# Joint Gram products of keys and queries in fewer TensorE visits, and masks and norms of the start handed to GpSimd

## The chip, the cores and the metric

The kernel runs on one core of a Trainium2 chip. The metric is the device time of one execution in microseconds (us), lower is better.

## The reference, cut to what matters

A linear attention with a delta rule runs over 768 time steps of 4 x 8 heads of size 48. Its output, 3072 rows of 384, goes through two feed-forward blocks one after the other ("MoE 1" with a product of two up projections, "MoE 2" with a leaky rectifier).

```python
for t in range(S):                       # attention, per batch b and head h
    kt, vt, bt = (k_n[:, :, t], v[:, :, t], beta[:, :, t, None])    # k_n: keys over their norms
    y[:, :, t] = np.einsum('bhd,bhde->bhe', q[:, :, t], state)
    v_old = np.einsum('bhde,bhd->bhe', state, kt)
    state = state + bt[:, :, :, None] * np.einsum('bhd,bhe->bhde', kt, vt - v_old)
x = y.transpose(0, 2, 1, 3).reshape(B * S, H * D)
x = (x @ w_a * (x @ w_b)) @ w_out                                   # MoE 1, 384 -> 1536 -> 384
h = x @ w_in                                                        # MoE 2, 384 -> 2048 -> 384
out = (np.maximum(h, 0.0) + alpha * np.minimum(h, 0.0)) @ w_out2
```

## The kernel before

**Stages.** Time is cut into six chunks (`c`, `NSC = 6`) of 128 time steps, each of two steps (`j`) of 64 time steps. In a chunk the recurrence becomes dense algebra for 32 (batch, head) pairs, 16 on each half of the partitions (`x`). A chunk `N` that comes next needs:

- `norms`: reciprocal norms of the keys, a chain of small operations over 128x32 elements (`ss`, `s`, `r` and `b` in the trace);
- `masks`: for each `j` the tile `mb`, 128x1024, beta times a triangular mask;
- Gram products `g` of keys with keys, masked into `ef`, and of keys with queries, masked into the rows of `Z` that `yp` reads later;
- `fold` (ScalarE copies in `ef`), then the triangular inversion (a transpose `eu<-ef` and a long chain of short VectorE operations on `inv`, `itmp`, `eu`), `diagonal` (transposes into `hw` and `TT`) and `offdiag` (32x32 products `w` and `xx`).

Then `step` runs once for each `j`: products `rp` (keys with the state) and a subtraction into `v`; products `up` and ScalarE copies into `SU`; products `sp` and a subtraction into the next `SU`; products `yp`, whose banks are split into `x`, the input of MoE 1. `up` and `sp` are done in two halves of eight heads, each half a "visit" of its own.

**Order of the work.** Chunk 0's attention and the inversions of chunks 0 and 1 come first; MoE 1 of chunk 0 starts once its `x` is there. From then on MoE 1 of chunk `c - 1` (128x512 matmuls `p` and `o`) runs on TensorE, and the small products of attention chunk `c` break into it, a visit at a time. The Gram products of chunk `c + 1` ride in the visits of `up` and `sp` as "mates" (`mate`): in the step of `j = 0` four visits take the key Grams of all heads, in the step of `j = 1` four visits take the query Grams. After chunk 5 come the rest of MoE 1 and MoE 2 (`h`, `o`). Operations are recorded first; `Schedule` then lists them greedily by engine, taking at each moment, of the operations that its cost table says are ready, the one with the longest path behind it. Consecutive small matmuls form one task; so a visit starts when the inputs and the banks of all its products are there.

**Engines.** Large matmuls take weights `wu`, which VectorE, ScalarE and GpSimd first decode (`raw`, `e`, `W`) and split in two (`wu`); the hidden activations `a` are split into `g` by ScalarE and GpSimd. Small products are 32-bit matmuls on tiles of the array: rows by the half of the partitions that is read, columns by the half of the bank that is written. Each shows as two MATMUL instructions in the trace, so that the eight heads of an `up` visit show as 32.

**Banks.** `chain` has two banks, `pre` and `g` one each. Mates use `chain` in chunk 1 and `pre` from chunk 2 on.

**What the change and the rows touch.** In the start: `A.masks(L, 0, ..., nc.vector)`, `A.masks(N, 0, ..., nc.vector)` and `A.norms(N, ef1)`, with `L` chunk 0 and `N` chunk 1. In the loop over `c`: `mate`, `step`, and the place of the third part of `norms` and of `masks`, which before stood inside the first step. In chunk 1 (`c == 1`, `direct` false) ScalarE copied the query Grams to `Z` and GpSimd masked them; from chunk 2 on VectorE did both in one operation per half.

Of the kernel before, what the change touches and what calls it, by code (L numbers as in the profile page):

```python
# [5 lines left out]
F32 = mybir.dt.float32  # L6
# [216 lines left out]
class Schedule:  # L223
# [24 lines left out]
    def costs(s, t):  # L248
        op, k = t.ops[0], len(t.ops)
        size = max(v.ix.size for v in ([op.dst] if op.dst is not None else []) + [v for v in op.src if v.ix.size < 2048])  # L250
        name = op.dst.tile.kw.get("name") if op.dst is not None else None
        t.rows = op.dst.p if op.dst is not None else None
        if t.dma:
            moved = op.dst if op.dst is not None else op.src[0]
            n = moved.ix.size * (moved.p[1] - moved.p[0])
            t.cost, t.lag = 0.42 if t.eng == SP_ else 0.1, 0.05 + n / (9.8e4 if name == "raw" else 6.5e4)
        elif t.eng == PE_:
            if t.large:
                t.cost = {512: 0.2267, 256: 0.12}[op.dst.ix.size]
            elif op.name == "transpose":  # L260
                t.cost = 0.09 * k
            else:
                rows = {0: 0.0, 1: 0.0}
                for x in t.ops:
                    a, b = x.src[0].p
                    for g in range(a // 64, (b + 63) // 64):
                        rows[g] += 0.00085 * x.src[0].ix.shape[-1]
                t.cost = max(0.0172 * k, *rows.values())
            t.lag = t.cost + 0.25
        elif t.eng == ACT_:  # L270
            t.lag = 0.16 + 0.00082 * size if any(map(in_psum, op.src)) else 0.19 + 0.00083 * size
            t.cost = t.lag + 0.02
        elif t.eng == POOL_:
            t.lag = 0.2 + 0.0007 * size
            if op.name == "tensor_tensor":
                t.lag = {32: 0.27, 384: 1.0, 512: 1.27, 768: 1.48, 1024: 1.91, 1536: 2.77}[size]
# [174 lines left out]
class Attention:  # L451
# [50 lines left out]
    def bank(s, name, tag="chain"):  # L502
        return s.pools[tag].tile([128, 512], F32, tag=tag, name=name, bufs=BANKS[tag])
# [95 lines left out]
            products(i)  # L599
        return g  # L600

    def mate(s, L, j, i8, tag, queries, then=None, direct=True):

        def begun():
            g, products = s.grams(L, j, i8, tag, *((1, 2) if queries else (0, 0)), go=False)

            def keep():
                if queries and direct:
                    s.mask_queries(L, j, i8, g, s.nc.vector)
                elif queries:  # L610
                    s.keep_queries(L, j, i8, g)
                    s.spend(ACT, 5)
                    s.mask_queries(L, j, i8, None, s.nc.gpsimd)
                else:
                    s.mask_keys(L, j, i8, g)
                    s.spend(DVE, 3)
                if then is not None:
                    then()

            return products, keep  # L620

        return begun
# [130 lines left out]
                    s.spend(ACT, 1.5)  # L753
            yield

    def step(s, c, j, L, mates=(), joined=False):

# [16 lines left out]

        if st > 0:
            rp = [bank("rp") for _ in halves]
            for i in range(8):
                for h, (o, _) in enumerate(halves):  # L780
                    near, far = slice(64 * h, 64 * h + 64), slice(64 - 64 * h, 128 - 64 * h)
                    nc.tensor.matmul(rp[h][near, i, :], Z[64:112, 0, o + i, :], SU[0][64:112, o + i, 0:48], start=True, stop=True)
                    nc.tensor.matmul(rp[h][far, i, :], Z[0:48, 0, o + i, :], SU[1][0:48, o + i, 0:48], start=True, stop=True)
            nc.vector.tensor_tensor(R[:, 0:8, :], rp[0], R[:, 0:8, :], ALU.subtract)
            s.spend(DVE, 2.3)
            if not joined:
                yield
            for x in range(2):
                sl, other = slice(64 * x, 64 * x + 64), slice(64 - 64 * x, 128 - 64 * x)
                nc.vector.tensor_tensor(R[sl, 8:16, :], rp[1][other], R[sl, 8:16, :], ALU.subtract)  # L790
                s.spend(DVE, 2.3)
            yield
        for o, hs in halves:
            up = bank("up")
            beside, keep = mate()
            for i in range(8):
                for x in range(2):
                    sl = slice(64 * x, 64 * x + 64)
                    nc.tensor.matmul(up[sl, i, :], s.TT[sl, j, o + i, :], R[sl, o + i, :], start=True, stop=True)
                beside(i)  # L800
            for x in range(2):
                sl = slice(64 * x, 64 * x + 64)
                nc.scalar.copy(SU[x][sl, hs, 0:48], up[sl])
                s.spend(ACT, 1.9)
            keep()
            yield
        for o, hs in halves:
            if st == 2 * NSC - 1:
                break
            sp = bank("sp")  # L810
            beside, keep = mate()
            for i in range(8):
                for x in range(2):
                    sl = slice(64 * x, 64 * x + 64)
                    nc.tensor.matmul(sp[64 * x : 64 * x + 48, i, :], bk[sl, j, o + i, :], SU[x][sl, o + i, 0:48], start=True, stop=True)
                beside(i)
            nc.vector.tensor_tensor(SN[1][0:48, hs, 0:48], SU[0][64:112, hs, 0:48], sp[0:48], ALU.subtract)
            s.spend(DVE, 4.4)
            nc.vector.tensor_tensor(SN[0][64:112, hs, 0:48], SU[1][0:48, hs, 0:48], sp[64:112], ALU.subtract)
            keep()  # L820
            yield
        tag = "chain" if c else "ab"
# [24 lines left out]
def attn_moe_kernel(tc, kt, qt, kn, vn, beta, w_a, w_b, w_o, w_in, w_o2, alpha, out):  # L847
    nc = tc.nc
    with ExitStack() as ctx:
# [249 lines left out]
        N = A.load(1)  # L1099
        al = cp.tile([128, M2], F32, name="al")  # L1100
        nc.sync.dma_start(al, alpha)
        A.masks(L, 0, wp.tile([128, 16, 64], F32, tag="w9", name="mb0"), nc.vector)
        A.masks(L, 1, xroom(0, 1, [16, 64], F32, "mb1"))
        A.scale_values(L, 0)
        A.clear()
# [25 lines left out]

# [147 lines left out]
        for c in range(NSC):  # L1279
# [3 lines left out]
            if c > 0:  # L1283
# [15 lines left out]
                for i, _ in enumerate(A.offdiag(L)):  # L1299
                    going = run(moe, fill, PIECE) and going  # L1300
                    if N is not None and i == 1:
                        norms = A.norms(N, late=True)
                        next(norms)
                        next(norms)
                mates = [[], []]

                def keys_done():
# [1 line left out]
                    A.scale_keys(N)  # L1309

                if N is not None:
                    after = {(0, 8): lambda: A.fold(N, 0), (1, 8): keys_done}
                    for q in range(2):
                        mates[q] += [A.mate(N, *jg, tag, q == 1, after.get(jg) if q == 0 else None, c > 1) for jg in HALF]
                closed.clear()
                L["y"] = [None, None]
                for j in range(2):
                    for i, _ in enumerate(A.step(c, j, L, mates[j], True)):
                        if N is not None and i == j == 0:
                            next(norms, None)  # L1320
                            A.masks(N, 0)
                            A.masks(N, 1)
# [191 lines left out]
```

## Time and profile before

| what | value |
|---|---|
| median of 3 runs | 1033.73 us (1033.64 to 1033.9) |
| profiled execution, its own time | 1034.53 us |
| its span, first to last instruction | 1032.8 us |
| mean granted TensorE clock | 0.973 of full speed |
| busy: PE, DVE, ACT, POOL | 981.1, 611.1, 480.6, 582.9 us |

PE is TensorE (matmuls), PEld its weight loads, DVE VectorE, ACT ScalarE, POOL GpSimd. In a timeline or a chain each row gives the start in us from the start of the span, the duration in us, the engine, the operation, output<-inputs and the number of instructions; in brackets stands the idle time of the engine before it and what ended it. A merged row of several instructions covers all of them.

### The profile page before, as it was taken

To read this page: it belongs to the slowest core of one execution; us is meant where nothing else is said; L and a number is where in the kernel's file an instruction comes from. 1 tells how busy PE (TensorE), PEld (TensorE's weight loads), DVE (VectorE), ACT (ScalarE), POOL (GpSimd) and SP (SyncE) were. 2 spreads that over 40 slices of the span, in tenths; PEclk is the share of its full clock that TensorE was granted. 3 is DMA by queue.
4 is the path that set the end of the run, shared out by engine and by line. 5 is a ranking of instruction groups with operands and counts; after the bars stand their busy time and mean duration, and the time that the engine had idled before them with its cause. 6 is when DMAs were issued, how large, how long until landed. Compare 5 with 4: busy or idle time off the path is not lost.

```text
span 1032.8 us, 24930 instructions
## 1 busy us (share of the span) xinstructions
PE 981.1 (95%) x10462; PEld 807.6 (78%) x10462; DVE 611.1 (59%) x1182; ACT 480.6 (47%) x963; POOL 582.9 (56%) x514
## 2 busy tenths in 40 slices
PE   6077999999999999999999999999999999999998
PEld 5076877887788788778878888888888888888886
DVE  8999766863684578358628799534343343433333
ACT  4386887565457554745567887212121121211211
POOL 7457999968466756756545998333333333333332
PEclk9559999999999999999999999999999999999999
DMA  9514343201300220000013751002020010000000
GB/s 249 182 42 139 110 145 111 78 1 34 95 32 2 63 95 1 18 19 32 16 35 98 235 172 62 31 1 62 0 62 1 1 62 1 28 4 1 31 0 31
DMA packets 26943, 61.47 MB, mean 60 GB/s; under 512 B 4304, under 2 KB 8912, under 8 KB 26832
## 3 DMA queue, kind: packets, MB, share of 16 engines
q1 hardware_dynamic: 26400, 59.50, 18.9%
q8 instruction: 82, 1.34, 0.5%
q10 hardware_dynamic: 432, 0.39, 0.1%
q14 instruction: 29, 0.24, 0.1%
HBM read 50.44 MB, written 9.44 MB: 58 GB/s over the span
## 4 chain that ended last, share of the span: by engine, by line
PE 83%; POOL 1%; issue 1%; ACT 0%; DVE 0%; DVEq 0%; POOLq 0%
PE o L201 32%; PE p L201 25%; PE h L201 19%; PE yp L201 2%; PE g L201 1%; PE up L201 1%; PE sp L201 1%; PE rp L201 1%; POOL wu L201 1%; PE xx L201 0%; PE w L201 0%; POOL W L201 0%; POOL g L201 0%; ACT SU L201 0%; ACT Z L201 0%
## 5 line engine op out<-in xcount | busy, mean ns | idle before, releaser
L201 PE MATMUL p<-x,wu 128*128 128x512 f32 x1296 | 321.9, 395 | 3.2 <-DVE a L201 1.3
L201 PEld LDWEIGHTS p<-x,wu 128*128 128x128 f32 x1296 | 239.0, 188 | 56.7 <-DVE a L201 1.7
L201 POOL TENSOR_TENSOR g<-neg,g 128x512 fp32r<-128x512 f32 x95 | 124.2, 1307 | 257.6 <-ACT g L201 257.6
L201 POOL TENSOR_TENSOR wu<-W,wu 128x384 fp32r<-128x384 f32 x195 | 202.1, 1041 | 98.3 <-ACT wu L201 97.2
L201 PE MATMUL o<-g,v 128*128 128x512 f32 x870 | 211.7, 388 | 0.0
L201 PE MATMUL h<-x,v 128*128 128x512 f32 x864 | 211.4, 389 | 0.0
L201 DVE TENSOR_SCALAR neg<-h,al 128x512 f32<-128x512 f32 (+1 forms) x97 | 72.2, 745 | 221.5 <-PE h L201 221.5
L201 ACT CAST g<-neg 128x512 fp32r<-128x512 f32 (+1 forms) x97 | 59.8, 616 | 301.5 <-DVE neg L201 283.9
L201 PEld LDWEIGHTS o<-g,v 128*128 128x128 f32 x870 | 162.4, 188 | 33.8 <-ACT x2s L201 0.5
L201 PEld LDWEIGHTS h<-x,v 128*128 128x128 f32 x864 | 162.2, 188 | 33.7
L201 PE MATMUL o<-g,wu 128*128 128x512 f32 x648 | 164.2, 394 | 0.1
L201 PEld LDWEIGHTS o<-g,wu 128*128 128x128 f32 x648 | 121.7, 189 | 26.8 <-POOL g L201 0.7
L201 ACT CAST wu<-W 128x384 fp32r<-128x384 f32 x216 | 110.2, 514 | 56.6 <-PE o L201 25.8
L201 POOL TENSOR_TENSOR g<-a,g 128x512 fp32r<-128x512 f32 x71 | 93.1, 1311 | 27.9 <-ACT g L201 27.7
L201 PE MATMUL g<-Z 48*64 48x64 f32 x1536 | 62.6, 241 | 34.0 <-DVE ef L201 22.6
L201 PEld LDWEIGHTS g<-Z 48*64 48x64 f32 x1536 | 56.8, 154 | 35.3 <-DVE ef L201 22.9
L201 DVE TENSOR_TENSOR a<-p,a 128x512 f32<-128x512 f32 x72 | 49.3, 685 | 55.2 <-PE p L201 49.4
L201 DVE TENSOR_TENSOR inv<-inv,itmp 128x240 f32<-128x240 f32 (+23 forms) x236 | 69.9, 296 | 13.6 <-ACT inv L201 6.5
L201 ACT COPY a<-p 128x512 f32<-128x512 f32 x72 | 42.2, 586 | 63.9 <-PE p L201 61.5
L201 DVE SCALAR_TENSOR_TENSOR neg<-h,neg 128x512 f32<-128x512 f32 (+1 forms) x97 | 66.5, 686 | 3.3
L201 ACT CAST g<-a 128x512 fp32r<-128x512 f32 x72 | 44.5, 618 | 19.9 <-DVE a L201 19.2
L201 POOL TENSOR_TENSOR f<-f,v 128x384 int32<-128x384 int32 x32 | 38.9, 1224 | 4.5 <-DVE v L201 3.4
(88 smaller groups left out, 960.1 us busy)
## 6 DMA issues: line engine op xcount, KB each, us to landing
v<-in_w_o_dram SPq DMA_DIRECT2D x16, 384.0 KB, 3.2
v<-in_w_in_dram SPq DMA_DIRECT2D x16, 384.0 KB, 3.6
k<-in_kn_dram SPq DMA_DIRECT2D x6, 768.0 KB, 5.3
Z<-in_kt_dram SPq DMA_DIRECT2D x24, 192.0 KB, 4.2
Z<-in_qt_dram SPq DMA_DIRECT2D x24, 192.0 KB, 4.1
raw<-in_w_a_dram SPq DMA_DIRECT2D x12, 384.0 KB, 3.9
v<-in_vn_dram SPq DMA_DIRECT2D x12, 384.0 KB, 3.7
raw<-in_w_b_dram SPq DMA_DIRECT2D x12, 384.0 KB, 4.9
```

The lines of the kernel that those rows point to most:

```text
L201: getattr(s.engines[op.eng], op.name)(*(real(x) for x in op.a), **{w: real(x) for w, x in op.k.items()})
```

## The change

Four parts.

1. `mate` now takes four heads and both Grams at once: one product with the keys as weights (64 columns) and keys beside queries as moving data (128 columns), in place of two with 64 each. There are still eight mates in a chunk, four in the step of each `j`, now with that `j`'s own heads. Behind each, VectorE does three mask operations (128x256 into `ef`, twice 64x256 into `Z`) in every chunk, chunk 1 too.
2. `step(..., wide=True)` from chunk 2 on: a mate rides with `rp`; the halves of `up` share one visit, with a mate; the halves of `sp` share one where there are no mates (chunk 5), else each half keeps its visit and mate. The second half of a joined visit is written to the other column half of its bank, so that four tiles of the array are in use. A step with mates goes from six visits to five, one without to four.
3. In the start the first masks of chunks 0 and 1 go from VectorE to GpSimd, and four operations of chunk 1's norms (`late=True`).
4. The planner gets a cost term for the columns that a tile of the array moves, and a GpSimd cost for 256 elements. Masks and the last part of the norms of the next chunk are recorded before the steps.

```diff
@@ Schedule.costs
-                rows = {0: 0.0, 1: 0.0}
+                rows, tiles = {0: 0.0, 1: 0.0}, {}
                 for x in t.ops:
                     a, b = x.src[0].p
                     for g in range(a // 64, (b + 63) // 64):
                         rows[g] += 0.00085 * x.src[0].ix.shape[-1]
-                t.cost = max(0.0172 * k, *rows.values())
+                        for c in range(x.dst.p[0] // 32, (x.dst.p[1] + 31) // 32):
+                            tiles[g, c] = tiles.get((g, c), 0.0) + 0.00085 * x.dst.ix.size
+                t.cost = max(0.0172 * k, *rows.values(), *tiles.values())
@@ Attention.mate
+            g = s.bank("g", tag).rearrange("p (i w n) -> p i w n", w=2, n=64)
+                for x, rows, both in ((0, slice(64, 112), slice(0, 2)), (1, slice(0, 48), slice(0, 3, 2))):
+                    nc.tensor.matmul(
+                        g[64 * x : 64 * x + 64, i], Z[rows, 0, i4 + i, :], Z[rows, both, i4 + i, :], start=True, stop=True,
+                    )
             def keep():
-                if queries and direct:
-                    s.mask_queries(L, j, i8, g, s.nc.vector)
-                elif queries:
-                    s.keep_queries(L, j, i8, g)
-                    s.mask_queries(L, j, i8, None, s.nc.gpsimd)
-                else:
-                    s.mask_keys(L, j, i8, g)
+                nc.vector.tensor_tensor(L["ef"][:, j * 16 + i4 : j * 16 + i4 + 4, :], g[:, :, 0, :], mb[:, hs, :], ALU.mult)
+                for x in range(2):
+                    nc.vector.tensor_tensor(Z[sl, 1 + x, hs, :], g[sl, :, 1, :], mb[sl, hs, :], ALU.mult)
@@ Attention.step
+            beside, keep = mate() if wide else none          # with rp
-        for o, hs in halves:
+        for group in (halves,) if wide else ((h,) for h in halves):              # up
+                for n, (o, _) in enumerate(group):
+                    for x in range(2):
+                        sl, at = slice(64 * x, 64 * x + 64), 64 * (x ^ n)
+                        nc.tensor.matmul(ups[n][at : at + 64, i, :], s.TT[sl, j, o + i, :], R[sl, o + i, :], start=True, stop=True)
-        for o, hs in halves:
+        for group in (halves,) if wide and not mates else ((h,) for h in halves):   # sp
@@ the start
-        A.masks(L, 0, wp.tile([128, 16, 64], F32, tag="w9", name="mb0"), nc.vector)
+        A.masks(L, 0, wp.tile([128, 16, 64], F32, tag="w9", name="mb0"))
-        norms = A.norms(N, ef1)
+        norms = A.norms(N, ef1, late=True)
-        A.masks(N, 0, xroom(1, 1, [16, 64], F32, "mb0"), nc.vector)
+        A.masks(N, 0, xroom(1, 1, [16, 64], F32, "mb0"))
@@ the loop over chunks
+                if N is not None:
+                    next(norms, None)
+                    A.masks(N, 0)
+                    A.masks(N, 1)
-                        mates[q] += [A.mate(N, *jg, tag, q == 1, after.get(jg) if q == 0 else None, c > 1) for jg in HALF]
+                        mates[q] += [A.mate(N, q, i4, tag, after.get((q, i4))) for i4 in range(0, 16, 4)]
-                    for i, _ in enumerate(A.step(c, j, L, mates[j], True)):
+                    for i, _ in enumerate(A.step(c, j, L, mates[j], True, c > 1)):
```

## Rows read from the trace of the kernel before

**Rows 1.** Busy time by stage: us, busy (instructions) of each engine, clock, DMA.

```profile
core 0: us, PE busy (x) PEld busy (x) DVE busy (x) ACT busy (x) POOL busy (x), PEclk, DMA share, GB/s
26.50:53.30 26.80, 3.60 (x66) 3.42 (x68) 24.86 (x67) 9.39 (x18) 10.88 (x6) 0.53 0.51 170
53.30:88.40 35.10, 26.38 (x935) 24.63 (x932) 32.40 (x75) 25.59 (x55) 22.68 (x20) 0.68 0.29 76
88.40:183.70 95.30, 91.60 (x1459) 72.44 (x1459) 68.42 (x129) 74.74 (x154) 87.73 (x86) 1.00 0.42 128
279.80:373.60 93.80, 93.80 (x1481) 76.01 (x1477) 59.68 (x142) 52.38 (x108) 61.30 (x57) 1.00 0.14 45
```

**Rows 2.** Timeline, first 27 us: VectorE, GpSimd, ScalarE rows of the start.

```profile
9.96 0.19 DVE L201 TENSOR_TENSOR r<-r,ss 128x32 f32<-128x32 f32 x1
...
11.52 1.90 POOL L201 TENSOR_TENSOR mb<-b,mask 128x1024 f32<-128x1024 f32 x1 [3.17 <-DVE b L201]
11.54 2.96 DVE L201 TENSOR_TENSOR mb<-b,mask 128x1024 f32<-128x1024 f32 x1
...
14.61 1.29 DVE L201 TENSOR_TENSOR ef<-g,mb 128x512 f32<-128x512 f32 x2
...
15.81 1.74 DVE L201 TENSOR_REDUCE ss<-ef 128x32 f32<-128x1536 f32 x1
...
17.47 1.27 DVE L201 TENSOR_TENSOR ef<-g,mb 128x512 f32<-128x512 f32 x2
...
19.32 1.24 ACT L201 COPY ef<-ef 32x512 f32<-32x512 f32 x2
...
20.66 2.74 DVE L201 TENSOR_TENSOR r<-r,s 128x32 f32<-128x32 f32 x1
...
23.32 1.94 DVE L201 STREAM_TRANSPOSE eu<-ef 128x1024 f32<-128x1024 f32 x1
```

**Rows 3.** Timeline, 45 to 54 us: VectorE late in the first inversion.

```profile
46.35 2.63 DVE L201 TENSOR_TENSOR mb<-b,mask 128x1024 f32<-128x1024 f32 x1
...
48.91 0.26 DVE L201 TENSOR_TENSOR itmp<-inv,eu 128x108 f32<-128x108 f32 x1
...
53.31 1.94 DVE L201 STREAM_TRANSPOSE hw<-inv 128x1024 f32<-128x1024 f32 x1
```

**Rows 4.** Timeline of TensorE where MoE 1 begins.

```profile
88.41 4.36 PE L201 MATMUL p<-x,wu 128*128 128x512 f32 x18 [0.66 <-DVE x L201]
...
97.40 2.33 PE L201 MATMUL p<-x,wu 128*128 128x512 f32 x9 [1.27 <-DVE a L201]
```

**Rows 5.** Chain that ended last, chunk 5: start, us, what, MATMUL instructions.

```profile
535.15 1.08 PE rp L201 x64
536.23 1.81 PE p L201 x7
538.04 1.06 PE up L201 x32
...
541.04 0.85 PE sp L201 x32
...
551.99 2.00 PE up L201 x64
...
555.80 1.93 PE yp L201 x128
```

**Rows 6.** The same chain in chunk 3: one visit of up with its mate.

```profile
324.81 2.04 PE o L201 x9
...
336.38 0.19 PE up L201 x2
...
337.47 2.27 PE p L201 x9
```

**Rows 7.** Waits of VectorE: us in total, times, longest.

```profile
DVE r L201 <- POOL r L201: 6.1, 3, 2.0
```

**Rows 8.** Groups of instructions by line, whole span: mean ns after the busy us.

```profile
L201 POOL TENSOR_TENSOR Z<-Z,mb 64x512 f32<-64x512 f32 x24 | 30.6, 1275 | 16.6 <-ACT Z L201 15.5
L201 DVE TENSOR_TENSOR Z<-g,mb 64x512 f32<-64x512 f32 x24 | 16.5, 689 | 15.6 <-PE g L201 15.3
```

**Rows 9.** Waits of TensorE: us in total, times, longest.

```profile
PE xx L201 <- issue: 1.0, 1, 1.0
```

**Rows 10.** Busy time by 5 us around that wait, at 234 us.

```profile
230.00:235.00 5.00, 4.21 (x141) 3.33 (x140) 2.40 (x4) 4.57 (x12) 2.67 (x4) 1.00 0.01 3
235.00:240.00 5.00, 4.82 (x15) 3.71 (x15) 1.12 (x3) 3.57 (x9) 4.42 (x7) 0.66 0.02 3
```

More of the change, by code (lines that the diff above doesn't have):

```diff
@@ L275, in costs @@
             if op.name == "tensor_tensor":
-                t.lag = {32: 0.27, 384: 1.0, 512: 1.27, 768: 1.48, 1024: 1.91, 1536: 2.77}[size]
+                t.lag = {32: 0.27, 384: 1.0, 256: 0.74, 512: 1.27, 768: 1.48, 1024: 1.91, 1536: 2.77}[size]
                 t.port = True
@@ L754, in offdiag, with step @@
             yield
-    def step(s, c, j, L, mates=(), joined=False):
+    def step(s, c, j, L, mates=(), joined=False, wide=False):
         nc, ap = s.nc, s.ap
@@ L783, in step @@
                     nc.tensor.matmul(rp[h][far, i, :], Z[0:48, 0, o + i, :], SU[1][0:48, o + i, 0:48], start=True, stop=True)
+                beside(i)
             nc.vector.tensor_tensor(R[:, 0:8, :], rp[0], R[:, 0:8, :], ALU.subtract)
@@ L791, in step @@
                 s.spend(DVE, 2.3)
+            keep()
             yield
-        for o, hs in halves:
-            up = bank("up")
+        for group in (halves,) if wide else ((h,) for h in halves):
+            ups = [bank("up") for _ in group]
             beside, keep = mate()
             for i in range(8):
-                for x in range(2):
[L798 to L804, printed above, removed]
+                for n, (o, _) in enumerate(group):
+                    for x in range(2):
+                        sl, at = slice(64 * x, 64 * x + 64), 64 * (x ^ n)
+                        nc.tensor.matmul(ups[n][at : at + 64, i, :], s.TT[sl, j, o + i, :], R[sl, o + i, :], start=True, stop=True)
+                beside(i)
+            for n, (_, hs) in enumerate(group):
+                for x in range(2):
+                    at = 64 * (x ^ n)
+                    nc.scalar.copy(SU[x][64 * x : 64 * x + 64, hs, 0:48], ups[n][at : at + 64])
+                    s.spend(ACT, 1.9)
@@ L805, in step @@
             keep()
             yield
-        for o, hs in halves:
+        for group in (halves,) if wide and not mates else ((h,) for h in halves):
             if st == 2 * NSC - 1:
                 break
-            sp = bank("sp")
+            sps = [bank("sp") for _ in group]
             beside, keep = mate()
             for i in range(8):
-                for x in range(2):
[L814 to L819, printed above, removed]
+                for n, (o, _) in enumerate(group):
+                    for x in range(2):
+                        sl, at = slice(64 * x, 64 * x + 64), 64 * (x ^ n)
+                        nc.tensor.matmul(sps[n][at : at + 48, i, :], bk[sl, j, o + i, :], SU[x][sl, o + i, 0:48], start=True, stop=True)
+                beside(i)
+            for n, (_, hs) in enumerate(group):
+                for x in range(2):
+                    at, old, new = 64 * (x ^ n), slice(64 - 64 * x, 112 - 64 * x), slice(64 * x, 64 * x + 48)
+                    nc.vector.tensor_tensor(SN[1 - x][new, hs, 0:48], SU[x][old, hs, 0:48], sps[n][at : at + 48], ALU.subtract)
+                    s.spend(DVE, 2.2)
@@ L1311, in attn_moe_kernel @@
                 if N is not None:
-                    after = {(0, 8): lambda: A.fold(N, 0), (1, 8): keys_done}
+                    after = {(0, 12): lambda: A.fold(N, 0), (1, 12): keys_done}
                     for q in range(2):
-                        mates[q] += [A.mate(N, *jg, tag, q == 1, after.get(jg) if q == 0 else None, c > 1) for jg in HALF]
+                        mates[q] += [A.mate(N, q, i4, tag, after.get((q, i4))) for i4 in range(0, 16, 4)]
                 closed.clear()
@@ L1317, in attn_moe_kernel @@
                 for j in range(2):
-                    for i, _ in enumerate(A.step(c, j, L, mates[j], True)):
[L1319 to L1322, printed above, removed]
+                    for i, _ in enumerate(A.step(c, j, L, mates[j], True, c > 1)):
                         going = run(moe, fill if j == 0 and i < 5 else fill2, PIECE) and going
```

15 lines of the change are left out of this document (11 added, 4 removed).

## The prediction

> **What bounds the kernel now.** I read the table of stages first, then the timeline of the start, then the chain that ended last, then the waits.
>
> The table [rows 1] shows two regimes. Until MoE 1 begins VectorE is the full engine: 24.86 of 26.8 us and 32.40 of 35.1 us busy, TensorE far below that. From 88.4 us on TensorE is the full engine: 91.60 of 95.3 us, then 93.80 of 93.8 us in a whole period of a chunk. GpSimd is close behind in the first of these stretches (87.73 of 95.3 us) and at two thirds in a later one. So there are two ways to gain: let MoE 1 begin earlier, or take TensorE time out of what follows.
>
> The start runs through masks, masked Grams `ef`, the fold, the transpose `eu`, the inversion, the transpose `hw` [rows 2, 3], and 35 us later the first `p` of MoE 1 at 88.41 us, which waited for VectorE's `x` [rows 4]. Two spots there are VectorE's own small operations. The first mask took VectorE 2.96 us beside GpSimd's 1.90 us; it ended at 14.50 us, 1.08 us after GpSimd's. A norm operation on 32 elements took 2.74 us, where the same kind takes 0.19 us before GpSimd is at work; it held back the transpose, though the fold was done at 20.56 us [rows 2]. In the middle of the inversion the second mask takes another 2.63 us [rows 3].
>
> In the TensorE part the chain [rows 5, 6] gives the price of each visit. `rp` takes 1.08 us, a half of `up` 1.06 alone and 1.09 with its mate (337.47 - 336.38), a half of `sp` 0.85, `yp` 1.93. Every visit also makes the next large matmuls late: nine after it take 2.27 us, nine elsewhere 2.04, so 0.23 us a visit [rows 6].
>
> **The change part by part: the start.** First the masks of chunk 0. Both on GpSimd, one after the other, they end at 11.52 + 1.90 = 13.42 and at 15.32 us. The first `ef` pair can start 1.08 us earlier, at about 13.5; the reduction (1.74) follows to 16.6; the second pair runs to 17.9 instead of 18.74; the fold (1.24) can end at 19.3 if ScalarE lets it go ahead of its other copies. The norm operations now stand in GpSimd's queue, so nothing long lies between fold and transpose: it starts at 19.4 at best, 3.9 us earlier. At worst the fold still ends at 20.56, which leaves 2.6 us, and VectorE, whose next norm step now waits for GpSimd, stalls with the transpose and the whole inversion queued behind it: such waits cost 6.1 us in three, 2.0 at most [rows 7], which leaves 0.6. I take 3.0, nearer to the upper end, since the norm step has ScalarE's copies to hide behind.
>
> Then the second mask on VectorE. The inversion stood from 46.35 to 48.91 us for it, 2.56 us [rows 3]; the four norm operations beside it are at 0.2 us each. Gone, this is 2.6 us; with one GpSimd wait of 2.0 in its place, 0.6. I take 2.6: GpSimd has 20 us to finish before this spot.
>
> What GpSimd takes over is two masks of 1.90 and four operations of some 0.25 us, 4.8 us. It is cost at nothing because GpSimd is busy 10.88 of 26.8 us in the stretch where most of it falls [rows 1]. Without that cover it would be 4.8 us on the way to MoE 1 (a rival below). From 53.31 to 88.41 us the same work is left, VectorE at 92%, so I move these 35.1 us as a block, and MoE 1 with them. Sum of the start: 5.6 us earlier (1.2 to 6.5).
>
> A rule speaks against this part. VectorE's two masks cost 2.96 and 2.63 us where GpSimd's cost 1.90 [rows 2, 3]. The Trainium skill, GPSIMD Engine Reference, section Engine selection, puts element-wise products on VectorE and calls GpSimd about twice as slow with two inputs; by it a mask alone on VectorE would be an estimated 0.95 us and the start would gain some 1.6 us less for each mask. No row shows VectorE alone at this, and beside a busy GpSimd it was the slower one here.
>
> **The visits.** How fast a tile of the array takes its small matmuls comes from [rows 5]. One half of `up` (32 instructions in two tiles, 16 each) takes 1.06 us, two halves in the same two tiles 2.00: 0.94/16 = 0.0588 us for an instruction, and 0.12 us to begin. `sp` gives (0.85 - 0.12)/16 = 0.046, `yp` in four tiles of 32 instructions (1.93 - 0.12)/32 = 0.057. Weights and moving columns are 64 and 48, 48 and 48, 32 and 64: the time follows the larger of the two at 0.0009 us a column. `rp` fills four tiles with 16 each in 1.08, so tiles run side by side. The rows show no instruction of 128 moving columns. If moving columns count, it takes 128 x 0.0009 = 0.112 us (0.118 as two of 64); if only weights do, 0.0588. I take 0.112, because of `yp`, whose weights are only 32 columns wide.
>
> Then merging saves next to nothing in a tile, and joining puts work on tiles that are already taken: the mate's two tiles are also those of one half of `rp` and of one half of the joined `up`. Such a visit lasts 0.12 + 16 x 0.0588 + 8 x 0.112 = 1.96 us. A visit of `sp` with a mate lasts 0.12 + 8 x 0.112 = 1.02, by its other tiles.
> - Chunks 2 to 4, a step without `yp`: before 1.08 + 4 x 1.09 + 5 x 0.23 = 6.59 us; after 2 x 1.96 + 2 x 1.02 + 4 x 0.23 = 6.88. Six steps: 1.7 us more.
> - Chunk 1, no joining: four visits 1.06 and four 1.02 for 1.09: 0.4 us less.
> - Chunk 5, no mates: first step 1.08 + 2 x 1.06 + 2 x 0.85 + 5 x 0.23 = 6.05 becomes 1.08 + 1.06 + 0.85 + 3 x 0.23 = 3.68; in the second `up` goes from 2.00 to 1.06. 3.3 us less.
>
> Sum 2.0 us less. At 0.118 it is 0.8 less; at 0.0588 visits of 1.53 and 0.85 give 5.5 + 1.1 + 3.3 = 9.9 less.
>
> **Cost at nothing.** Mask operations of the mates: 24 a chunk, of half the size of one of 0.689 us [rows 8], so 8.3 to 16.5 us, for 12 x 0.69 = 8.3 before. VectorE is busy 59.68 of 93.8 us in such a period and 68.42 of 95.3 us in chunk 1 [rows 1], where it takes over from ScalarE and GpSimd; GpSimd loses 8 x 1.275 = 10.2 us there [rows 8]. If that cover were gone in chunk 1, up to 13 us of VectorE would stand before TensorE's visits. The last mates of a chunk now hold key Grams too, so the next inversion begins some 4 us later; `w`, which needs it, has several us in hand. The planner's term and the earlier recording of masks and norms move orders only; no DMA is added or moved. A stall of 0.96 us for no shown reason [rows 9], and a clock of 0.66 in the 5 us after it [rows 10], which is 1.7 us at 1.2 in place of 2.4 GHz, may vanish or come twice: 2.7 us either way, not counted.
>
> **The sum.** 1034.53 - 5.6 - 2.0 = 1026.9 us for the profiled execution. That one lies 0.8 above the median of the runs, so 1026.1 us.
>
> **Rivals.**
> 1. The start gains nothing: VectorE's free time fills with decoding and the second inversion, and `x` comes when it came. For it: VectorE has such work at hand all along. Against it: both waits stood in the very chain to `hw`, where each operation needs the last. 1034.53 - 2.0 - 0.8 = 1031.7.
> 2. Slower: GpSimd sets the stretch after 88.4 us. It is idle there for only 7.6 of 95.3 us [rows 1]. If the 4.8 us handed to it push its decoding past the start of MoE 1 the gain of 5.6 is lost and TensorE waits for weights: 1034.53 + 4.8 - 2.0 - 0.8 = 1036.5. It decides once that much of its work lands behind the first `p`. Against it: 15.9 us idle between 26.5 and 53.3.
> 3. The merged Gram costs a tile less than two single ones, at the limit as one (0.0588): 1034.53 - 5.6 - 9.9 - 0.8 = 1018.2. `yp` speaks against it, though its tiles share their rows. The Trainium skill, TensorEngine Tiling, section Instruction Overhead, gives each matmul some 60 cycles on top of its columns; by it the merged one would be an estimated three quarters of two, and the whole 1021.1. `sp`, faster than `up` with as many moving columns, disagrees with a fixed floor.
>
> **How the numbers follow.** Forecast 0.66, rival 1 0.13, rival 2 0.09, rival 3 0.12. The forecast's own range is 1024.2 (6.5 and 3.0 gained) to 1031.7 (1.2 and 0.8). Widened to half of rival 3 and over rival 1, the range is 1019.0 to 1032.5. A change under 0.2%, 2.1 us, can't be told from none: rival 1 and a sliver of the forecast are the same, 0.14; rival 2 is slower, 0.09; the rest faster, 0.77.
>
> **What would show it.** In the start: both first masks on GpSimd, `eu` transposed near 20 us, `hw` near 48, the first `p` near 83. Visits of 1.96 us for `rp` and `up` with mates, 1.02 for `sp`, three small visits in chunk 5's first step before `yp`. A period of chunk 3 of 93.8 + 0.6 us. Wrong it would be by a first `p` still near 88, by new waits of `p` for `wu`, or by wide visits near 1.5 us.

## The result and the profile after

| | before | after |
|---|---|---|
| median of 4 runs each | 1033.68 us (1031.12 to 1033.9) | 1021.34 us (1021.01 to 1021.72) |
| span of the profiled execution | 1032.8 us | 1019.1 us |
| mean granted TensorE clock | 0.973 | 0.977 |
| busy: PE, DVE, ACT, POOL | 981.1, 611.1, 480.6, 582.9 us | 977.5, 610.0, 477.4, 574.7 us |

The ratio is 0.9886, 95% interval 0.9872 to 0.9899: 12.3 us faster in the medians. The forecast was 1026.1 us (7.6 less than the median shown then), range 1019.0 to 1032.5. Direction and range held; 4.8 us of gain were not forecast. Between the profiled spans the gain is 13.7 us, 6.1 more than the forecast's 7.6. The forecast's own range was 1024.2 to 1031.7 us, and the time lies below it; it is inside the stated range only because that one was widened toward rival 3, which e4 rules out below.

Times are medians of undisturbed executions: one of e8 (1300.98 us) and one of the kernel before beside e5 to e8 (5462.3 us) are left out.

Stages of the changed kernel, cut at the same events as [rows 1], same columns:

```profile
22.10:46.50 24.40, 6.39 (x161) 6.15 (x158) 22.34 (x64) 11.47 (x22) 17.60 (x14) 0.64 0.78 232
46.50:81.00 34.50, 26.79 (x935) 25.01 (x932) 32.48 (x76) 25.61 (x55) 22.12 (x20) 0.64 0.28 78
81.00:176.30 95.30, 94.11 (x1317) 73.83 (x1321) 71.40 (x140) 69.49 (x144) 89.60 (x87) 1.00 0.42 128
276.50:371.00 94.50, 94.50 (x1350) 77.00 (x1348) 60.23 (x154) 52.96 (x109) 61.48 (x58) 1.00 0.15 44
```

The first inversion takes 24.4 us for 26.8, the stretch up to MoE 1 hardly less than before, a period of a chunk 94.5 for 93.8. In the 95.3 us behind the first `p` TensorE now works 94.11 us for 91.60, so it waits 2.5 us less. Another 2.7 us of unforecast gain lie in chunk 2, as the table of places below shows.

Timeline of the start after (rows of GpSimd, VectorE, ScalarE), as [rows 2]:

```profile
11.25 3.76 POOL L201 TENSOR_TENSOR mb<-b,mask 128x1024 f32<-128x1024 f32 x2 [2.90 <-DVE b L201]
12.89 1.75 DVE L201 TENSOR_REDUCE ss<-ef 128x32 f32<-128x1536 f32 x1 [1.72 <-ACT ef L201]
14.56 2.48 DVE L201 TENSOR_TENSOR ef<-g,mb 128x512 f32<-128x512 f32 x4
14.97 2.76 POOL L201 TENSOR_TENSOR k<-k,b 128x1536 f32<-128x1536 f32 x1
15.93 2.50 ACT L201 COPY ef<-ef 32x512 f32<-32x512 f32 x4 [1.03 <-DVE ef L201]
...
18.57 0.25 POOL L201 TENSOR_TENSOR r<-r,s 128x32 f32<-128x32 f32 x1
...
18.85 0.18 DVE L201 TENSOR_SCALAR r<-r 128x32 f32<-128x32 f32 x1 [0.69 <-POOL r L201]
18.95 1.95 DVE L201 STREAM_TRANSPOSE eu<-ef 128x1024 f32<-128x1024 f32 x1
```

The transpose `eu` starts at 18.95 us for 23.32, with one wait of 0.69 us for GpSimd's `r` ahead of it. VectorE does the reduction first and then all four mask products in one go, another order than the prediction had in mind.

TensorE where MoE 1 begins, as [rows 4]:

```profile
81.04 6.38 PE L201 MATMUL p<-x,wu 128*128 128x512 f32 x27 [0.70 <-DVE x L201]
87.94 3.58 PE L201 MATMUL p<-x,wu 128*128 128x512 f32 x13 [0.52 <-DVE a L201]
92.04 2.35 PE L201 MATMUL o<-g,wu 128*128 128x512 f32 x9 [0.52 <-DVE TT L201]
```

The first `p` comes 7.37 us earlier, and the two waits behind it are 0.52 + 0.52 us for 1.00 + 1.27.

Chain that ended last, chunk 5 after, as [rows 5]:

```profile
523.40 1.08 PE rp L201 x64
...
527.44 1.08 PE up L201 x64
...
531.24 0.87 PE sp L201 x64
...
534.83 1.93 PE yp L201 x128
```

Both halves of `up` in four tiles take 1.08 us where one took 1.06 and two in two tiles 2.00; `sp` 0.87 where each half took 0.85. Three visits ahead of `yp`, as forecast. And the visits with mates, as first rows of the large matmuls around them in TensorE's timeline of chunk 3:

```profile
327.53 0.33 PE L201 MATMUL rp<-SU,Z 48*64 48x48 f32 x8
...
329.47 1.20 PE L201 MATMUL o<-g,wu 128*128 128x512 f32 x4
...
332.88 0.38 PE L201 MATMUL up<-v,TT 64*64 64x48 f32 x10
...
334.84 1.88 PE L201 MATMUL p<-x,wu 128*128 128x512 f32 x7
...
336.66 0.25 PE L201 MATMUL sp<-SU,k 64*48 64x48 f32 x2
...
337.69 0.50 PE L201 MATMUL p<-x,wu 128*128 128x512 f32 x1
```

`rp` with a mate 1.94 us, joined `up` with a mate 1.96, `sp` with a mate 1.03 (forecast 1.96, 1.96, 1.02). The waits of TensorE from 81 us on, as [rows 9], are these three and no other over 0.2 us:

```profile
PE p L201 <- DVE x L201: 0.7, 1, 0.7
PE o L201 <- DVE TT L201: 0.5, 1, 0.5
PE p L201 <- DVE a L201: 0.5, 1, 0.5
```

Where the 13.7 us between the two spans went, each worked out from the starts of TensorE's rows:

| place | forecast | measured |
|---|---|---|
| start, up to `eu` (23.32 to 18.95) | 3.0 | 4.4 |
| first inversion, `eu` to `hw` (29.99 to 27.60) | 2.6 | 2.4 |
| `hw` to first `p` (35.10 to 34.49) | 0 | 0.6 |
| visits: their lengths 0.1 more, eight fewer (67 to 59) at 0.23 | 2.0 | 1.7 |
| stall in `xx` of chunk 2, 1.1, and the slow clock behind it, 1.6 | not counted | 2.7 |
| waits in the first 108 large matmuls of MoE 1 | 0 | 0.9 |
| waits for `wu` and `SU` in chunk 1 | 0 | 1.0 |

### The profile page after: what moved, and what is told of

Same layout as the page of the kernel before. It is cut to its first block, busy times and chain, and to the rows that moved or that the text cites. A ratio compares the mean times of both kernels' runs of the same rounds, so it can differ in the third digit from the quotient of the medians.

```text
span 1019.1 us, 23984 instructions
## 1 busy us (share of the span) xinstructions
PE 977.5 (96%) x9950; PEld 805.1 (79%) x9950; DVE 610.0 (60%) x1232; ACT 477.4 (47%) x955; POOL 574.7 (56%) x512
## 4 chain that ended last, share of the span: by engine, by line
PE 91%; DVE 5%; ACT 1%; issue 1%; DMA 1%; SPq 0%; DVEq 0%; POOL 0%; ACTq 0%
PE o L201 34%; PE p L201 29%; PE h L201 19%; PE up L201 2%; PE yp L201 2%; PE g L201 2%; DVE itmp L201 1%; DVE inv L201 1%; PE rp L201 1%; PE sp L201 1%; DMA k<-in_kn_dram 1%; PE xx L201 1%; PE w L201 1%; DVE raw L201 1%; DVE ef L201 0%
## 5 line engine op out<-in xcount | busy, mean ns | idle before, releaser
L201 PE MATMUL p<-x,wu 128*128 128x512 f32 x1296 | 318.0, 394 | 1.4 <-DVE x L201 0.7
L201 PE MATMUL g<-Z 48*64 48x64 f32 (+1 forms) x1024 | 66.4, 275 | 27.9 <-DVE ef L201 17.9
L201 PEld LDWEIGHTS g<-Z 48*64 48x64 f32 x1024 | 50.6, 160 | 28.9 <-DVE ef L201 18.2
```

The source lines that it names most:

```text
L201: getattr(s.engines[op.eng], op.name)(*(real(x) for x in op.a), **{w: real(x) for w, x in op.k.items()})
```

## The experiments

Theory A: the terms of the table add up, the start's come from its masks and norms, the visits' from eight visits fewer and moving columns, and the stalls come and go with something else. The rivals stand in each expectation. All were timed beside the kernel before, in four groups (e1 to e4, e5 to e8, e9 to e11, e12); ratios are to it. Its own median was 1033.96, 1032.45, 1032.10 and 1032.14 us in these groups, so a difference of some 2 us between medians of two groups proves little; where ratios are compared, it is their intervals that count.

**The two halves of the change alone.**

```diff
# e1: the kernel before, with
+        A.masks(L, 0, wp.tile([128, 16, 64], F32, tag="w9", name="mb0"))
+        norms = A.norms(N, ef1, late=True)
+        A.masks(N, 0, xroom(1, 1, [16, 64], F32, "mb0"))
# e2: the changed kernel, with
+        A.masks(L, 0, wp.tile([128, 16, 64], F32, tag="w9", name="mb0"), nc.vector)
+        norms = A.norms(N, ef1)
+        A.masks(N, 0, xroom(1, 1, [16, 64], F32, "mb0"), nc.vector)
```

> The kernel before with only the start changed: first masks of chunks 0 and 1 and four norm operations on GpSimd. Theory A (the start shifts MoE 1 as a block, whatever the visits do): first p near 81 us, 7.4 us earlier than 88.41, and 1026.3 us. Theory B (part of the 12.3 us comes only from start and visits together): clearly less, near 1030. If the 0.96 us stall at xx and the slow clock behind it are a matter of luck, the time can be 2.7 us lower in either case.

1024.21 us, ratio 0.9913 (0.9896 to 0.9929). `eu` at 19.27, `hw` at 46.88, first `p` at 81.72 us: the start alone brings MoE 1 forward by 6.7 us, and the short waits behind the first `p` (0.49 + 0.52) come with it. There are waits of 0.39 for `a` at 140 us and 1.00 for `wu` at 142 us and a stall of 0.91 put down to issue at 226 us.

> The changed kernel with the start put back as it was before: merged Grams and joined visits alone. Theory A: the visits and their 0.23 us after each are worth 1.7 us, which gives 1032.0; 1029.3 if the stall at xx is absent. Theory B (the relief of GpSimd in chunk 1 removes TensorE's waits there, 2 us more): 1027 to 1030. First p again near 88.

1029.69 us, ratio 0.9965 (0.9952 to 0.9978). First `p` at 88.21 and the waits of 1.00 and 1.27 behind it as before; the visits are those of the changed kernel; no wait for `SU` or `wu` in chunk 1, no stall in `xx`, one of 0.99 at 164 us. So the relief in chunk 1 comes with the visits. The time fits the additive reading without the `xx` stall. The product of the two ratios is 0.9878, the whole change 0.9886. That alone is no clean sum, since both halves lack the `xx` stall of the kernel before. In the spans e1 gains 9.9 us and e2 4.7; without the 2.7 us of that stall and with their own stalls (0.91 and 0.99) put back they are worth 8.1 and 3.0. With 2.7 for the stall this makes 13.8 of the 13.7 us: the halves add up.

**Join only where there are no mates.**

```diff
-                    for i, _ in enumerate(A.step(c, j, L, mates[j], True, c > 1)):
+                    for i, _ in enumerate(A.step(c, j, L, mates[j], True, c == NSC - 1)):
```

> The changed kernel with joined visits in chunk 5 alone, so that in chunks 2 to 4 rp has no mate and each half of up and sp keeps its visit with one mate. Theory A (a mate beside four busy tiles costs its full tile time): a step falls from 1.965 + 1.958 + 2 x 1.034 + 4 x 0.228 = 6.90 to 1.079 + 2 x 1.065 + 2 x 1.034 + 5 x 0.228 = 6.42 us, six steps 2.9 us, so 1018.4 us. Rival (fewer visits are what pays): one visit more in each of six steps, 1.4 us, so 1022.7.

1019.56 us, ratio 0.9868 (0.9851 to 0.9884), 1.8 us under the changed kernel, but the intervals of the two overlap. Its small visits, with 0.23 us for each, sum to 3.0 us less than the changed kernel's, as theory A had it (2.9). From the first `p` to the end its span is only 1.1 us shorter (936.9 us for 938.0); stalls of 1.00 us in `xx` at 227 us and 0.20 in `g` eat part of the rest. By these rows, and by e10 below, joining with mates costs time in chunks 2 to 4; the gain of the visits is that of chunk 5 and of chunk 1.

**Two products of 64 columns in place of one with 128.**

```diff
-                for x, rows, both in ((0, slice(64, 112), slice(0, 2)), (1, slice(0, 48), slice(0, 3, 2))):
-                    nc.tensor.matmul(g[64 * x : 64 * x + 64, i], Z[rows, 0, i4 + i, :], Z[rows, both, i4 + i, :], ...)
+                for w in range(2):
+                    for x, rows in ((0, slice(64, 112)), (1, slice(0, 48))):
+                        nc.tensor.matmul(g[64 * x : 64 * x + 64, i, w, :], Z[rows, 0, i4 + i, :], Z[rows, w * (1 + x), i4 + i, :], ...)
```

> The changed kernel with each merged Gram product of 128 moving columns written as two of 64 with the same weights. Theory A (moving columns set a tile's pace): 16 instructions of 0.058 in place of 8 of 0.111 us, visits 0.03 to 0.06 us longer, 1.4 us in all, so 1022.7. Rival (weights set the pace, so that merging saves a load): 8 more instructions of 0.058 in the mates' tiles, 0.47 us in each of 12 wide visits and less in the others, so 1028 to 1030.

1024.38 us, ratio 0.9915 (0.99 to 0.993). The `rp` visit of chunk 3 in its timeline:

```profile
327.96 0.33 PE L201 MATMUL rp<-SU,Z 48*64 48x48 f32 x8
...
329.96 1.65 PE L201 MATMUL p<-x,wu 128*128 128x512 f32 x6
```

2.00 us, joined `up` 2.01, `sp` 1.09: 0.05 to 0.06 us a visit more than merged, 1.6 us over all. The other 1.4 us of the difference to the changed kernel stand beside stalls of 0.98 (`g`, 162.1 us) and 0.81 (`xx`, 227.8 us). A merged product costs a tile nearly what two single ones cost.

**Norms back on VectorE.**

```diff
-        norms = A.norms(N, ef1, late=True)
+        norms = A.norms(N, ef1)
```

> The changed kernel with one part undone: the norms of chunk 1 back on VectorE. Theory A, the masks and the norms each gave part of the 4.4 us by which the transpose `eu` came earlier: one 32-element norm operation on VectorE is held up beside GpSimd's work again, for 2 to 3 us between the fold and the transpose, `eu` starts at 21 to 22 us instead of 18.95, the first `p` at 83 to 84 instead of 81.04, and the time is 1023.3 to 1024.3 us. Rival, the masks alone did it and the norm operation now falls into VectorE's idle time: `eu` within 0.5 us of 18.95 and 1021.0 to 1021.8 us.

1025.91 us, ratio 0.9927 (0.9915 to 0.9939). Its start, GpSimd's and VectorE's rows:

```profile
14.97 2.77 POOL L201 TENSOR_TENSOR k<-k,b 128x1536 f32<-128x1536 f32 x1
18.42 0.19 DVE L201 TENSOR_TENSOR r<-r,s 128x32 f32<-128x32 f32 x1
19.07 1.27 POOL L201 TENSOR_TENSOR Z<-Z,mb 64x512 f32<-64x512 f32 x1 [1.33 <-ACT Z L201]
19.13 1.85 DVE L201 STREAM_TRANSPOSE eu<-ef 128x1024 f32<-128x1024 f32 x1
```

And two windows where its MoE 1 begins, the clock being the first figure behind POOL's:

```profile
81.00:90.00 9.00, 8.00 (x27) 6.16 (x27) 8.76 (x23) 4.80 (x9) 6.67 (x6) 0.81 0.83 258
90.00:100.00 10.00, 8.35 (x30) 6.73 (x31) 9.46 (x15) 7.53 (x14) 7.50 (x7) 0.83 0.14 40
```

Theory A failed here: the operation that took 2.74 us before takes 0.19, because it falls into a pause of GpSimd, and `eu` starts only 0.18 us later. Up to `eu` the masks alone did it. The time is still 4.6 us over the changed kernel, and neither theory said so. The rows show where: stalls of 0.91 and 0.97 us put down to issue in `yp` at 68.7 and 76.8 us, so the first `p` at 81.88 though `hw` came at 45.57; waits of 1.91 for `x` and 1.78 for `a`; and behind each of these two some 3.4 us at half the clock (granted 0.81 and 0.83 in the windows). So the first `p` comes 0.84 us later than in the changed kernel, the first 108 large matmuls of MoE 1 take 31.2 us for 27.9, and there are a stall of 0.90 us in `yp` at 161 us and a wait of 0.27 for `wu`: 5.3 of the 5.6 us between the two spans. What the norms' place has to do with these waits and stalls was not tried; the time of this run does not price it.

**First masks back on VectorE.**

```diff
-        A.masks(L, 0, wp.tile([128, 16, 64], F32, tag="w9", name="mb0"))
+        A.masks(L, 0, wp.tile([128, 16, 64], F32, tag="w9", name="mb0"), nc.vector)
-        A.masks(N, 0, xroom(1, 1, [16, 64], F32, "mb0"))
+        A.masks(N, 0, xroom(1, 1, [16, 64], F32, "mb0"), nc.vector)
```

> The changed kernel with one part undone: the first masks of chunk 0 and of chunk 1 back on VectorE. Theory A, each was on the path: `eu` some 1.1 us later (20.0), and the second mask stands in the inversion for 2.6 us, `hw` at 50 instead of 46.55, the first `p` at 84.5 to 85, 1024.6 to 1025.4 us. Rival, only the second mask mattered, since with the norms on GpSimd the fold is held up by other things: `eu` at 19, 1023.5 to 1024.0 us. Second rival, the masks are worth nothing without the norms' move: 1021.3 us.

1025.73 us, ratio 0.9924 (0.991 to 0.9938). Its two masks on VectorE, GpSimd's rows beside the first and its last row ahead of the second:

```profile
11.25 1.90 POOL L201 TENSOR_TENSOR mb<-b,mask 128x1024 f32<-128x1024 f32 x1 [2.90 <-DVE b L201]
11.27 2.96 DVE L201 TENSOR_TENSOR mb<-b,mask 128x1024 f32<-128x1024 f32 x1
13.11 3.74 POOL L201 TENSOR_TENSOR k<-k,b 128x1536 f32<-128x1536 f32 x1
...
38.58 2.76 POOL L201 TENSOR_TENSOR k<-k,b 128x1536 f32<-128x1536 f32 x1
...
43.90 1.22 DVE L201 TENSOR_TENSOR mb<-b,mask 128x1024 f32<-128x1024 f32 x1
```

`eu` at 20.68 (+1.73), `hw` at 49.45 (1.17 more behind `eu`), first `p` at 83.70, and the two waits behind it are back at 1.03 and 1.31. So the masks carry the start. The waits at MoE 1 come back with them here, but masks alone do not settle these: e5, with its masks on GpSimd, waits longer. The same mask took 2.96 us beside GpSimd and 1.22 alone. Beside GpSimd it ends 1.08 us after GpSimd's mask does (14.23 for 13.15), as in the kernel before, and GpSimd's next product `k` takes 3.74 us for the 2.76 that it takes with no mask of VectorE beside it. So the two engines seem to wait for each other, and moving the mask also took 0.98 us off GpSimd, which the prediction did not count.

**Chunk 1's query masks back on ScalarE and GpSimd.**

```diff
+                    if tag == "chain":
+                        nc.scalar.copy(Z[sl, 1 + x, hs, :], g[sl, :, 1, :])
+                        s.spend(ACT, 2.5)
+                        nc.gpsimd.tensor_tensor(Z[sl, 1 + x, hs, :], Z[sl, 1 + x, hs, :], mb[sl, hs, :], ALU.mult)
+                        s.spend(POOL, 2.9)
+                        continue
                     nc.vector.tensor_tensor(Z[sl, 1 + x, hs, :], g[sl, :, 1, :], mb[sl, hs, :], ALU.mult)
```

> The changed kernel, but in chunk 1 the query masks go by ScalarE copies and GpSimd products as before the change (VectorE has 8 x 2 products fewer, GpSimd as many more). Theory A, the relief of GpSimd is what took away the waits of TensorE for `wu`, `SU` and `a` between 130 and 180 us (0.29 + 0.72 + 0.22 us before; 1.0 + 0.39 with the start alone): waits of 1 to 1.5 us return there and the time is 1022.3 to 1023.0 us. Rival, the joint Grams' order or the earlier start took them away: no wait over 0.2 us there and 1021.0 to 1021.8 us.

1020.91 us (1020.42 to 1021.24), ratio 0.9877 (0.9863 to 0.9891); no wait over 0.2 us between 81 and 180 us. The rival holds: GpSimd's relief in chunk 1 is not what took the waits away, and no gain from it shows. This run does not price it finer than some 1 us, since its profile differs where MoE 1 begins:

```profile
80.81 10.96 PE L201 MATMUL p<-x,wu 128*128 128x512 f32 x40 [1.71 <-DVE x L201]
```

The two waits of 0.52 behind the first `p` are absent, but the granted clock is 0.50 from 81.4 to 84.8 us. The waits for `SU` went with the new visits (e2 has none either).

**Moving TensorE's instruction blocks.** The stalls put down to issue stand at another place in each kernel. All 15 of over 0.75 us after 60 us, over all traces of this study, begin between 0.03 us before and 0.54 us after the moment at which a transfer on the DMA queue for instructions has landed. That a load which comes too late causes them was still a guess. In e8, e9, e10 and e12 products of the start are issued twice, so that the position of all later instructions in their blocks moves (e10 has the edit of e3 too; e11 has the edits of e3 and e7 and issues nothing twice).

```diff
+            grams += op.name == "matmul" and op.dst.tile.kw.get("name") == "g"
+            for _ in range(2 if op.name == "matmul" and op.dst.tile.kw.get("name") == "g" and 128 < grams <= 160 else 1):   # e12: <= 144
                 getattr(s.engines[op.eng], op.name)(...)
```

> The kernel before, in which 32 of the Gram products of the start are issued twice, at a time when TensorE is mostly idle; the order of everything else stays as it was. TensorE's instructions come in blocks: 82 transfers of 16.4 KB for 21,073 rows, 257 rows a block, and each stall of some 1 us that the profile puts down to issue begins where such a transfer has just landed. The 32 doubled products move every later instruction by about 128 rows, half a block. Theory A, the stalls come from where the blocks end: the stalls of 1.42 us at 84 us (`yp`) and of 0.96 us at 234 us (`xx`) vanish or stand at other places, with the 1.7 us of slow clock behind the second; the time is anywhere between 1029.5 (none left) and 1034 (as many elsewhere). Rival, they belong to the bursts themselves: both stalls stand within 1 us of where they stood, with the same lengths, and the time is that of the kernel before or up to 0.3 us more.

1031.45 us, ratio 0.9985 (0.9974 to 0.9996). The stall in chunk 2 is gone; one of 1.22 us stands in `xx` of chunk 3, with a slow clock behind it. Rows of its timeline, two of the start and two of the burst:

```profile
17.72 3.94 POOL L204 TENSOR_TENSOR Z<-Z,mb 64x512 f32<-64x512 f32 x3 [0.85 <-ACT Z L204]
20.40 1.31 DVE L204 TENSOR_TENSOR r<-r,s 128x32 f32<-128x32 f32 x1
...
324.31 1.15 PE L204 MATMUL xx<-TT,hw 32*32 32x32 f32 x113
326.68 0.29 PE L204 MATMUL xx<-TT,hw 32*32 32x32 f32 x15 [1.22 <-issue]
```

The DMA view of 324.0 to 325.3 us, 40 slices, bytes booked where a transfer begins, and its one packet:

```profile
GB/s 0 504 0 0 0 0 0 0 0 0 0 0 0 0 0 0 0 0 0 0 0 0 0 0 0 0 0 0 0 0 0 0 0 0 0 0 0 0 0 0
...
q8 instruction: 1, 0.02, 5.7%
```

The window behind, as [rows 10]:

```profile
325.00:330.00 5.00, 3.78 (x80) 2.99 (x68) 2.25 (x3) 3.69 (x10) 4.42 (x6) 0.76 0.01 2
```

The block begins to load in the second slice, 0.28 us ahead of the burst, and lands at 325.21; TensorE has done 113 of 128 products by 325.47 and waits. In the start `r` took 1.31 us, up to the end of GpSimd's three `Z` (21.66): `eu` came at 21.63 and the first `p` at 86.26, and the stall of 1.42 us in `yp` at 84 us is one of 0.45. So the doubled products moved the start too, and the shorter time is the start's: from the first `p` to the end it is 944.4 us, as in the kernel before. What e8 shows is that the stall moves with the block; its time shows no more.

> The changed kernel with the same 32 Gram products of the start issued twice, everything else in its order: all later instructions of TensorE move by about 128 rows, half a block. The profiled execution of the changed kernel has no stall put down to issue after 81 us. Theory A, that is where its blocks happen to end, no property of the joint visits: one or two stalls of 0.4 to 1.2 us come up in bursts of small products (`xx`, `yp`, `g`), with a slow clock behind where the stall is long, and the time is 1022 to 1025 us. Rival, the joint visits leave no room for them: no such stall after 81 us, 1020.9 to 1021.8 us.

1021.62 us (1020.97 to 1022.05), ratio 0.9894 (0.9877 to 0.991). One stall of 0.38 us at 178 us, no slow clock: nearer to the rival; the changed kernel stands at both positions.

> The version that joins visits in chunk 5 alone, with the same 32 Gram products issued twice. Its profile has a stall of 1.0 us in `xx` at 227 us and smaller ones. Theory A: that stall goes to another place or away; 1017.5 us with none left, 1021 with one long one and a slow clock behind it. Rival, the stall belongs to this `xx` burst: it stands at 227 us again, 1019.3 to 1019.9 us.

1017.64 us (1017.12 to 1018.02), ratio 0.9856 (0.9842 to 0.9871), the fastest of all. The `xx` burst of chunk 2 in its timeline:

```profile
226.15 1.29 PE L204 MATMUL xx<-TT,hw 32*32 32x32 f32 x128
```

And in the timeline of e3, the same kernel with its blocks unmoved:

```profile
226.15 1.15 PE L201 MATMUL xx<-TT,hw 32*32 32x32 f32 x113
228.31 0.29 PE L201 MATMUL xx<-TT,hw 32*32 32x32 f32 x15 [1.00 <-issue]
```

Same burst, same start (first `p` at 81.05 and 81.04 us), and only the place in the block differs: 2.0 us between the spans, 1.9 between the medians. The two were timed in different groups, and the intervals of their ratios overlap; that of e10 lies just under the changed kernel's.

> A candidate from two results: visits joined in chunk 5 alone (1.8 us faster than the changed kernel), and chunk 1's query masks by ScalarE copies and GpSimd products (0.4 us faster than the changed kernel, not told apart from no change). If both hold side by side, 1018.8 to 1019.4 us; if the second was only chance, 1019.6; if instruction blocks end badly, 1 to 3 us more, with a stall of some 1 us put down to issue in the profile.

1019.57 us (1018.98 to 1021.38), ratio 0.9878 (0.9863 to 0.9894). Its profiled execution is the slowest of its four and has the stall and the slow clock again, in its timeline and in the window behind:

```profile
228.17 0.29 PE L201 MATMUL xx<-TT,hw 32*32 32x32 f32 x16 [1.26 <-issue]
```

```profile
228.90:232.30 3.40, 3.40 (x9) 2.63 (x9) 0.00 (x0) 3.07 (x9) 2.84 (x4) 0.50 0.02 5
```

The median is that of e3 (1019.56): chunk 1's query masks add no gain. One kernel's executions differ by 2.4 us; the other three had no profile, so that the stall comes and goes between them is likely, not shown.

> The kernel before with 16 of the Gram products of the start issued twice, so that later instructions move by about 64 rows, a quarter of a block. In the bursts of `xx` so far (five in each of twelve kernels) a stall inside the burst came only where an instruction block began to load between 0.6 and 0.1 us ahead of the burst: in chunk 2 of the kernel before (0.09 ahead), in chunk 3 when it was moved by half a block (0.28 ahead). Theory A, by a quarter block the load of chunk 2 falls further ahead and those of the other chunks into their bursts: no stall in any `xx`, no slow clock after 100 us, 1029.8 to 1031.3 us; then some 2 to 3 us of the gain measured for the change are where the blocks end. Rival, some burst always meets a block so: one stall of about 1 us with the slow clock behind it, 1031.5 to 1034 us, and the gain of the change holds at any position of the blocks.

1030.91 us, ratio 0.9981 (0.9969 to 0.9993). First `p` at 88.40 as before, no stall in any `xx`, the clock full from 87.3 us on:

```profile
233.04 1.29 PE L204 MATMUL xx<-TT,hw 32*32 32x32 f32 x128
```

From the first `p` to the end 941.9 us for 944.4. The ratio makes it 2.0 us (0.7 to 3.2), the medians 1.2 (1030.91 for 1032.14). So some 1.2 to 2.5 us of what the change seemed to gain were the position of the blocks. Against this version the change would be worth an estimated 9.8 us (0.9886/0.9981 of 1032), still more than the forecast 7.6.

## Why the prediction was right, point by point

- **Start, up to `eu`: right in place, too small, and half wrong in cause.** It took 3.0 us, at best 3.9; measured 4.4, of which 0.27 is the masks' own earlier start (11.25 for 11.52). The masks were the cause, as said. That a norm operation of 2.74 us had to leave VectorE was not: e5 keeps it there, and it takes 0.19. It was long only while GpSimd worked (2.74, 1.31 and 0.19 us in the kernel before, e8 and e5). With both masks in GpSimd's queue one after the other, GpSimd's pause falls where the norm operation runs. The feared wait for GpSimd's `r` was 0.69 us, for 2.0.
- **Second mask in the inversion: right** (2.6 forecast, 2.4 measured). But e6 shows 1.22 for the same mask at the same place when GpSimd is idle, so the price was GpSimd's neighbourhood rather than VectorE's own. In the kernel before this mask too ended 1.07 us after a mask of GpSimd (48.98 for 46.01 + 1.90 = 47.91).
- The Trainium skill, GPSIMD Engine Reference, section Engine selection, puts such products on VectorE; the text's estimate by it was 0.95 us alone. e6 shows 1.22 us alone, 2.96 beside GpSimd, and 1.90 on GpSimd: the page's order holds for VectorE alone, by a factor of 1.56 and not 2, and the rows decide for this start.
- **`hw` to `p` as a block: right** within 0.6 us.
- **Visits: right.** 1.94 to 1.96 and 1.03 us for 1.96 and 1.02; 1.7 us in all for 2.0 (the 3.0 that the range allows for the visits has no working in the text). Moving columns count, as `yp` had said. Rival 3 is out: e4's two products cost only 0.05 us a visit more than one merged. The Trainium skill, TensorEngine Tiling, section Instruction Overhead, taken as 60 cycles on top of the columns of each matmul, would have made the merged product an estimated three quarters of two. The runs disagree with that reading: a merged instruction takes (1.95 - 0.12 - 16 x 0.0588)/8 = 0.111 us, and the 0.05 us of e4 over the 8 instructions of a tile in a visit make 0.117 for two, so 0.95.
- **What failed: "a stall of 0.96 us for no shown reason ... not counted", and waits of TensorE costed at nothing.** Together 4.6 us that the sum left out; most of the other 1.5 of the 6.1 are the start's 1.4. The stall and its clock (2.7) vanished where no block of instructions begins to load just ahead of that `xx` burst (0.09 us ahead of its start in the kernel before, 1.8 us behind it in the changed one): e10 and e12 move the blocks with the first `p` within 0.01 us, and the stall goes; in e8 it moves to chunk 3. Such a load does not always stall the burst, so this part of the gain is luck, as the prediction's "may vanish or come twice" allowed; without it the median would be an estimated 1024.0 us, at the edge of the forecast's own range. The 0.9 at MoE 1 comes back when the masks do (e6), but e5 and e7, with the masks on GpSimd, have other waits there, so its cause is only partly shown. The 1.0 in chunk 1 went with the visits (e2), not with GpSimd's relief (e7). Of these waits the prediction's rows show the stall and the 1.27 us for `a` [rows 4, 9], and it priced only what lies on the way to the first `p`.
- **Rival 1** (the start gains nothing) and **rival 2** (GpSimd sets the stretch) did not come: 7.4 us earlier, and GpSimd idle for 5.7 of 95.3 us with no wait of `p` for `wu`.

Joining the visits of chunks 2 to 4 was forecast to cost 1.7 us against the old visits. Against unjoined visits with merged Grams its rows cost 3.0 us (e3), and the version without it takes 1017.64 us with its blocks moved (e10).

Open: why TensorE waits so long at MoE 1 in e5, why half of the bursts that a block meets do not stall, and what decides whether the clock falls behind a stall (it did after 0.96 us in the kernel before, not after 1.00 in e3).

## What to carry to other kernels

Price an operation by who else is at work in that moment, not by its engine alone: the mask was 1.22 or 2.96 us on VectorE and 1.90 on GpSimd, and it made GpSimd's next product longer too. Sum up the waits of the bound engine in the whole span before a forecast, and ask of each whether the change moves its cause. Where an engine that runs short instructions in bursts is the bound, a gain of 0.2% can be the place where its instruction blocks end: time a second version with the stream moved before crediting the edit.

## What was unexpected of the hardware

- TensorE's instructions are loaded in blocks of 16.4 KB on a DMA queue of their own: 82 for 21,073 rows before, 78 for 20,072 after, 257 rows a block in both. An `xx` burst is 128 matmuls and their weight loads in 1.29 us. In 70 such bursts (14 kernels, the five after MoE 1 has begun in each) a block began to load between 0.7 us ahead of the burst's start and 0.1 us behind it 12 times; five of these stalled inside, by 0.81 to 1.26 us, one just behind (0.91), and none of the other 58 did.
- The granted clock fell to 0.5 (1.2 of 2.4 GHz) for 3.4 us behind waits of 1.91 and 1.78 us (e5) and 1.71 us (e7) and behind stalls in small products of 0.96, 1.22 and 1.26 us; it stayed at 1.0 after waits of 1.34 and 1.31 us (e6) and 1.41 us (e4) where MoE 1 begins, and after the stall of 1.00 us in e3.
- An operation of VectorE on 128x32 elements took 0.19 us in a pause of GpSimd, and 0.93, 1.31 and 2.74 us where it ended within 0.05 us of the end of a GpSimd product beside it. Not every operation is held so: one of the inversion, `itmp` on 128x84, took 0.24 us beside GpSimd's mask in the changed kernel and 0.24 with GpSimd idle before.
